# Gate and value projections as seven block products in one pass over 576-token batches, in a fused attention and feed-forward kernel

## The chip, the cores and the metric

The kernel runs on one core of a Trainium2 chip. A core has TensorE (PE; PEld are its weight loads), VectorE (DVE), ScalarE (ACT), GpSimd (POOL) and SyncE (SP), which issues most DMAs. Each engine works through its own queue in order and waits for others by semaphores. The metric is the device time of one execution in microseconds (us), the median of several runs.

## What is computed

Eight batches of eight heads with 576 tokens go through a linear attention. Its output, laid out as 4608 tokens of 512 features, goes through a gated feed-forward block:

```python
def phi(x):
    proj = np.einsum('bhsd,df->bhsf', x, w_phi)
    proj = proj - np.max(np.abs(proj), axis=-1, keepdims=True)
    return np.concatenate([np.exp(proj), np.exp(-proj)], axis=-1)
q_p, k_p = (phi(q), phi(k))
kv = np.einsum('bhsf,bhsd->bhfd', k_p, v)
z = np.sum(k_p, axis=2)
num = np.einsum('bhsf,bhfd->bhsd', q_p, kv)
den = np.einsum('bhsf,bhf->bhs', q_p, z)[..., None] + 1e-06
attn = num / den
...
rms = np.sqrt(np.mean(x * x, axis=-1, keepdims=True) + 1e-06)
xn = x / rms * rms_g
g = xn @ w_gate
silu = g * (1.0 / (1.0 + np.exp(-g)))
val = xn @ w_val
return (silu * val @ w_out).astype(np.float32)
```

`w_gate` and `w_val` are 512 x 1536, `w_out` is 1536 x 512.

## The kernel before

Every operand of the large products is split in two (`_split`): ScalarE casts it to a reduced format ("hi"), and VectorE or GpSimd computes the remainder ("lo"). A product then takes three matmuls in place of one: hi x hi, hi x lo, lo x hi. The weights come in as 64-bit floats and are decoded (`_decode`) by ScalarE, VectorE and GpSimd to 32-bit ones, which go to DRAM (`wgs`, `wvs`, `wos`).

There are three stages, one after the other, with DRAM buffers between them.

1. **Attention** (`front`, `mid`, `back`, `last`), 32 pairs of heads as a software pipeline. It writes its output, transposed, to `xs`. In its gaps lies **fill** (`fill`, called from the loop over the pairs by `landed` and `load_x`): for blocks of T = 384 tokens that are ready, the first three of the twelve 128-wide slices of gate and value are computed from the unnormalised x, with weights `wf1`, and stored in `gvs`. Ten of the twelve blocks are filled there, two (`tail`) in the next stage. One unit of fill is twelve matmuls of 384 columns, a copy by ScalarE and a store.
2. **Gate/value**, the loop over `bk` (12 blocks of 384 tokens) and `j` (nine remaining slices). `gv(bk, j)` computes gate and value of a slice by twelve matmuls each (four parts of the 512 features, three matmuls per part), into banks `fp` and `gp`. `hidden` applies Silu on ScalarE, the product on VectorE, and stores to `hs`. `gv_raw` loads one of the three filled slices back from `gvs`, scales it by the norm `ri` and stores it the same way. `prep` makes the norm of the next block: squares on ScalarE and sums on GpSimd in turn, two matmuls with ones for the sum over partitions, root on ScalarE, reciprocal on VectorE, scaling by g and ri on VectorE, and the split into one of three buffers `xo`. It is called four or two units into a block for the block after. The weights of slice j+1 are loaded and split during the first block (`load_gv`, DMAs issued on ScalarE); the decoding of `w_out` runs in later blocks.
3. **Output** (from `hload`): 18 groups of 256 tokens. The product with `w_out` is done as 2 x 2 blocks by seven block products instead of eight, a scheme of Strassen and Winograd. `load_o` makes the combined weights (four block differences `wc` on VectorE, then splits `wh`, `wl`), `operands` the combined inputs (a11, a12, s1 to s4, a22), and `omm` issues one product of 18 matmuls of 256 columns. Four of the six weight sets are made in stage 2, two at the start of stage 3.

The order on each engine is set by the framework: it takes the instructions in the order in which the program names them and moves later ones forward where its own timing model says that they would be ready. The helper `late()` holds against that: an instruction issued inside it may not stand ahead of the last earlier instruction on its engine (ScalarE, VectorE, GpSimd).

## Time and profile before

| | us |
|---|---|
| median of 3 runs | 1379.31 (1377.8 to 1383.53) |
| the profiled execution | 1376.67 |
| its span, first to last instruction | 1374.9 |
| first and last gate/value matmul | 567.4, 1087.3 |
| first matmul of the output stage | 1097.3 |

The mean granted TensorE clock is 0.976. Rows of the profile read like this: a group has its line, engine and operation, then output <- inputs by the program's names, partitions x elements, the count, the busy time and the mean of one in ns, and the idle time of the engine ahead of it with what ended it. In the view of one line or tile, the three numbers after the count are the shortest, the median and the longest in ns, followed by the first and the last start in us. A timeline row is start, length, engine, line, operation, with the count of instructions merged into it; the step from one start to the next tells the pace, since matmuls overlap. The chain is the work that ended last, followed back through what released it.

### The profile page before, as it was taken

The numbers are of one execution on the slowest core, as the hardware profiler recorded it, in microseconds if no ns is written. First come the engines' busy times: TensorE is split into PE (matmuls) and PEld (weight loads), VectorE is DVE, ScalarE is ACT, GpSimd is POOL, SyncE is SP. The second block draws the span as 40 slices with busy tenths as digits, with TensorE's granted clock in tenths as the row PEclk, the third lists the DMA queues.
The fourth block names the chain that finished last, engine by engine and source line by source line (L and its number), as shares of the span: only waits on it lengthen the run. The fifth ranks groups of instructions, "written<-read, shape, count | busy, mean of one in ns | idle before, by whom it ended". The sixth has DMA issues, their size and how long they took to land.

```text
span 1374.9 us, 24771 instructions
## 1 busy us (share of the span) xinstructions
PE 1300.6 (95%) x9108; PEld 1284.4 (93%) x9108; DVE 880.2 (64%) x1293; ACT 713.3 (52%) x1490; POOL 605.5 (44%) x580
## 2 busy tenths in 40 slices
PE   7988999999999899889999999999999789999998
...
GB/s 165 123 139 127 153 185 149 163 141 171 151 188 153 149 154 119 157 194 129 144 97 167 140 155 132 127 140 157 147 127 98 162 122 127 135 173 131 151 149 47
DMA packets 198953, 197.18 MB, mean 143 GB/s; under 512 B 69104, under 2 KB 180848, under 8 KB 198832
## 3 DMA queue, kind: packets, MB, share of 16 engines
...
q8 instruction: 72, 1.18, 0.4%
...
## 4 chain that ended last, share of the span: by engine, by line
PE 65%; DMA 14%; DVE 12%; issue 3%; ACT 2%; POOL 2%; SPq 1%; ACTq 0%; DVEq 0%; POOLq 0%
PE fp L575 9%; PE gp L575 9%; PE fp L472 7%; PE gd L742 5%; PE gy L742 5%; PE gz L742 5%; PE acc L352 5%; DMA x<-xs 5%; DMA gvr<-gvs 3%; PE sm L416 3%; PE fp L742 3%; PE fp L416 2%; PE pp L314 2%; PE pp L312 2%; PE pp L313 2%
## 5 line engine op out<-in xcount | busy, mean ns | idle before, releaser
L575 PE MATMUL fp<-xo,wg 128*128 128x384 f32 x1296 | 247.4, 339 | 14.7 <-ACT sl L560 14.5
L381 POOL TENSOR_TENSOR ql<-eq,qh 128x256 fp32r<-128x256 f32 x256 | 218.5, 884 | 83.7 <-issue 48.6
L575 PE MATMUL gp<-xo,wv 128*128 128x384 f32 x1296 | 246.6, 338 | 6.3 <-DVE wv L61 5.2
L575 PEld LDWEIGHTS fp<-xo,wg 128*128 128x128 f32 x1296 | 229.2, 190 | 18.0 <-ACT sl L560 17.9
L575 PEld LDWEIGHTS gp<-xo,wv 128*128 128x128 f32 x1296 | 230.3, 191 | 7.3 <-DVE wv L61 5.6
L316 DVE TENSOR_REDUCE mx<-pp 128x4 f32<-128x512 f32 (+1 forms) x160 | 101.1, 633 | 62.8 <-PE pp L314 61.4
L352 PE MATMUL acc<-vm,ek 128*128 128x65 f32 x1024 | 132.5, 268 | 0.0
L560 ACT ACTIVATE sl<-fp 128x384 f32<-128x384 f32 x108 | 52.6, 487 | 153.1 <-PE fp L575 126.2
L54 POOL TENSOR_TENSOR wa<-raw,wa 128x192 f32<-128x192 f32 (+1 forms) x112 | 65.1, 601 | 150.9 <-DVE wa L52 70.3
L562 DVE TENSOR_TENSOR h<-sl,gp 128x384 f32<-128x384 f32 x108 | 59.1, 549 | 110.6 <-PE gp L575 67.6
L352 PEld LDWEIGHTS acc<-vm,ek 128*128 128x128 f32 x1024 | 129.0, 193 | 0.0
L61 POOL TENSOR_TENSOR xo<-x,xo 128x768 fp32r<-128x768 f32 x24 | 44.6, 1878 | 190.7 <-ACT xo L60 190.7
L377 ACT ACTIVATE qh<-sm 128x512 fp32r<-128x512 f32 (+1 forms) x192 | 96.6, 503 | 0.0
L472 PE MATMUL fp<-xo,fg 128*128 128x384 f32 x432 | 90.8, 346 | 3.2 <-ACT xo L60 3.0
L312 PE MATMUL pp<-wh,th 128*128 128x256 f32 x288 | 89.2, 311 | 3.3 <-DVE yr L319 2.1
L376 ACT ACTIVATE eq<-sm 128x512 f32<-128x512 f32 x128 | 78.1, 610 | 17.3 <-PE sm L365 16.8
L583 DVE TENSOR_TENSOR gvr<-gvr,ri 128x768 f32<-128x768 f32 x36 | 38.0, 1056 | 72.7 <-DMA gvr<-gvs 72.7
L314 PE MATMUL pp<-wh,tl 128*128 128x256 f32 x288 | 84.2, 299 | 0.0
L313 PE MATMUL pp<-wl,th 128*128 128x256 f32 x288 | 82.0, 286 | 0.0
L472 PEld LDWEIGHTS fp<-xo,fg 128*128 128x128 f32 x432 | 75.6, 192 | 4.2 <-ACT xo L60 3.3
L472 PE MATMUL fp<-xo,fv 128*128 128x384 f32 x360 | 77.1, 346 | 0.7 <-ACT nd L418 0.7
L383 POOL TENSOR_TENSOR ql<-eqr,qh 128x256 fp32r<-128x256 f32 x32 | 24.7, 772 | 119.0 <-ACT qh L377 119.0
...
## 6 DMA issues: line engine op xcount, KB each, us to landing
...
```

Of the source, the lines that this page charges most:

```text
L312: nc.tensor.matmul(o, th[:, cs], wh, start=True, stop=False)
L313: nc.tensor.matmul(o, th[:, cs], wl, start=False, stop=False)
L314: nc.tensor.matmul(o, tl[:, cs], wh, start=False, stop=True)
L316: nc.vector.tensor_reduce(mx[:, 0:2 * m], pp[:, 0:2 * m], axis=AX.X, op=ALU.max, apply_absolute_value=True)
L352: nc.tensor.matmul(acc[:, sg, h], e[h][:, sg, j], vm[:, h, j], start=False, stop=(h == 1 and j == T0 - 1))
L376: nc.scalar.activation(ei[:, sg], yi, AF.Exp, scale=1.0 - 2.0 * sg)
L377: nc.scalar.activation(hi[:, sg], yi, AF.Exp, scale=1.0 - 2.0 * sg)
L381: nc.gpsimd.tensor_tensor(lo[:, sg, cs], ei[:, sg, cs], hi[:, sg, cs].bitcast(F32), ALU.subtract)
L416: nc.tensor.matmul(o[:, 0:SH], a[:, h, sg], e[:, sg, h, cs], start=(i == 0), stop=(i == 5))
L472: nc.tensor.matmul(fp, w, xx[x][:, c], start=(i == 0), stop=(i == 3 * NC - 1))
L575: nc.tensor.matmul(gp[:, 0:T], w, e[:, c], start=(i == 0), stop=(i == 3 * NC - 1))
L742: nc.tensor.matmul(place[n], a[:, kp], w[:, o], start=(first and kp == 0 and i == 0), stop=(kp == KP - 1 and i == 2), skip_group_check=True)
```

## The change

Stage 2 is replaced. A block is now a whole batch, T2 = 576 tokens, as two halves of T = 288, and a unit computes gate and value of one slice for all 576 tokens at once. Of the matrix [gate, value] by [first, second half of the features] by [first, second half of the tokens] the same seven block products are formed as in stage 3: seven products of six matmuls with 288 columns in place of four times twelve for the same area. The combined weights of all nine slices are made once, in the first batch (`combos`), and stay on chip in fixed places (`home`), 18 tiles of 7 x 256 columns. Partial sums gather in a bank `x` by accumulation, with ScalarE taking snapshots between products (`snap`), and banks `y` and `z` are added on VectorE (`plus`). The last two products of a unit (3 and 4) are issued among the first ones of the next unit.

The combined inputs of the next batch are made around the border of two batches into single buffers, each as soon as the last product that reads the old one is past. The norm of the next batch (`norm`) is issued in `late()` after unit 7 of nine; its sums are on VectorE now, and squares, their sum and `ri` have one buffer each. Fill works on blocks of 288: 14 in the attention stage, two in the first batch; its splits are inside `late()`, and two blocks can be loaded ahead. The raw slices come back in pieces of 288 tokens, six a batch, with one buffer. The decoding of `w_out` is done as twelve pieces of 512 columns in batches 1 to 6, each right behind its load. The weight sets of stage 3 take the places of used gate/value weights in the last batch, whose slices go in the order `LAST`. In stage 3 the remainder of s2 moves from GpSimd to VectorE, the other four are halved, and s2 and s4 are formed in place.

```diff
-    T = 384
+    T = 288
+    T2 = 2 * T
     NB = N // T
     KP = NJ // 2
     DH = DM // 2
-    CH = 256
...
+    SLOT = [128, 7, DH]
+    rga = ctx.enter_context(tc.tile_pool(name="rga", bufs=1, side="right"))
+    slot = lambda n, i, pool: pool.tile(SLOT, F32R, name=f"w{'hl'[i]}{n}")
+    flat = lambda t, n: t.rearrange("p a b -> p (a b)")[:, 0:n]
+    wf1 = [[flat(slot(7 + wi, i, rga), NC * J1 * 128).rearrange("p (c j) -> p c j", c=NC) for i in range(2)] for wi in range(2)]
...
+    def norm(x, bank):
+        ss = xm.tile([128, T2], F32, name="ss")
+        for c in range(NC):
+            sq = ss if c == 0 else xm.tile([128, T2], F32, name="sq")
             nc.scalar.activation(sq, x[:, c], AF.Square)
+            if c:
+                nc.vector.tensor_tensor(ss, ss, sq, ALU.add)
+        ri = xm.tile([128, T2], F32, name="ri")
+        for b in range(2):
+            bs = slice(b * T, (b + 1) * T)
+            s2 = xm.tile([128, 2, T], F32R, name="sq")
+            _split(nc, s2[:, 0], s2[:, 1], ss[:, bs])
+            sp = bank()[:, 0:T]
+            nc.tensor.matmul(sp, ones, s2[:, 0], start=True, stop=False)
+            nc.tensor.matmul(sp, ones, s2[:, 1], start=False, stop=True)
+            nc.scalar.activation(ri[:, bs], sp, AF.Sqrt, scale=1.0 / DM, bias=eps)
+            nc.vector.reciprocal(ri[:, bs], ri[:, bs])
         for c in range(NC):
             nc.vector.scalar_tensor_tensor(x[:, c], x[:, c], g[:, c:c + 1], ri, ALU.mult, ALU.mult)
+        return ri
...
-            else:
-                units.extend(fill(bk, *halves(x)))
+            xo = px.tile([128, 2, NC, T], F32R, name="xo")
+            with late():
+                units.extend(fill(bk, *halves(x, xo[:, 0], xo[:, 1])))
...
         if i == PR - 6:
-            fills.insert(0, None)
+            xn = fetch(0)
+        if i == PR - 3:
+            with late():
+                ri = norm(xn, lambda: ps_f.tile([128, T], F32, name="fp"))
...
+    def combos(n, w, t):
+        sub = lambda o, a, b: nc.vector.tensor_tensor(t[:, o], a, b, ALU.subtract)
+        sub(0, w[:, 3], w[:, W11])
+        sub(2, w[:, W22], w[:, 3])
+        sub(1, w[:, W22], t[:, 0])
+        sub(3, w[:, W21], t[:, 1])
+        wh, wl = home(n, 0), home(n, 1)
+        _split(nc, wh[:, 0:3], wl[:, 0:3], w[:, 0:3])
+        _split(nc, wh[:, 3:7], wl[:, 3:7], t)
+        return wh, wl
+    def stage_gv(j):
+        js = slice((J1 + j) * 128, (J1 + j + 1) * 128)
+        w, t = (stg.tile([128, 4, DH], F32, name="wc") for _ in range(2))
+        for src, os in ((wgs, (W11, W21)), (wvs, (3, W22))):
+            v = src[:, js].rearrange("(k c p) j -> k p c j", k=2, p=128)
+            for k, o in enumerate(os):
+                nc.scalar.dma_start(out=w[:, o].rearrange("p (c j) -> p c j", c=2), in_=v[k])
+        return w, t
+    def decode_o(job):
+        src, n, keep = job
+        raw, tmp = (stg.tile([128, 4, DH], F32, name="wc").rearrange("p a b -> p (a b)") for _ in range(2))
+        if src.dtype == F32:
+            nc.sync.dma_start(out=raw[:, 0:n], in_=src)
+            keep(raw[:, 0:n])
+            return
+        nc.sync.dma_start(out=raw.bitcast(I32), in_=src.bitcast(I32))
+        with late():
+            keep(_decode(nc, None, raw.bitcast(I32).rearrange("p (n t) -> p n t", t=2), n, tmp))
...
+    def operands(a11, a12, a21, a22, tile_of, tmp):
+        ops, t = {}, {}
+        def split(name, x, lo):
+            h, l = tile_of(name)
+            nc.scalar.copy(h, x)
+            m = x.shape[1] // 2
+            for c in (slice(0, m), slice(m, 2 * m)) if lo is nc.gpsimd else (slice(0, 2 * m),):
+                lo.tensor_tensor(l[:, c], x[:, c], h[:, c].bitcast(F32), ALU.subtract)
+            ops[name] = h, l
+        def sums():
+            t["s3"] = tmp()
+            nc.vector.tensor_tensor(t["s3"], a11, a21, ALU.subtract)
+            nc.vector.tensor_tensor(a21, a21, a22, ALU.add)
+            nc.vector.tensor_tensor(a11, a21, a11, ALU.subtract)
+        def second():
+            split("s2", a11, nc.vector)
+            nc.vector.tensor_tensor(a12, a12, a11, ALU.subtract)
+        return ops, [lambda: split("a11", a11, nc.vector),
+                     lambda: (split("a12", a12, nc.vector), sums()), second,
+                     lambda: split("s3", t["s3"], nc.gpsimd), lambda: split("s1", a21, nc.gpsimd),
+                     lambda: split("s4", a12, nc.gpsimd), lambda: split("a22", a22, nc.gpsimd)]
+    def product(n, ops, w, out, start):
+        (xh, xl), o = ops[OPS[n][0]], OPS[n][1]
+        i = 0
+        for c in range(2):
+            for a, e in ((w[0], xh), (w[0], xl), (w[1], xh)):
+                nc.tensor.matmul(out, a[:, o, c * 128:(c + 1) * 128], e[:, c], start=(start and i == 0), stop=(i == 5),
+                                 skip_group_check=True)
+                i += 1
+    class Unit:
+        def __init__(self, p, j, ops, w):
+            self.p, self.j, self.ops, self.w = p, j, ops, w
+        def mm(self, n):
+            out, start = {1: ("x", True), 2: ("z", True), 6: ("x", False), 7: ("y", True), 5: ("x", False),
+                          3: ("x", False), 4: ("y", False)}[n]
+            if start:
+                t = ps_f.tile([128, T], F32, name="fp") if out == "x" else ps_g.tile([128, 512], F32, name="g" + out)
+                setattr(self, out, t[:, 0:T])
+            product(n, self.ops, self.w, getattr(self, out), start)
+            getattr(self, f"done{n}", lambda: None)()
+        def snap(self, name, bufs=1):
+            t = gw.tile([128, T], F32, name=name, bufs=bufs)
+            nc.scalar.copy(t, self.x)
+            return t
+        def plus(self, ps, s, name, bufs=1):
+            t = gw.tile([128, T], F32, name=name, bufs=bufs)
+            nc.vector.tensor_tensor(t, ps, s, ALU.add)
+            return t
+        def store(self, b, x, y, eng):
+            h = gw.tile([128, T], F32, name="h", bufs=3)
+            eng.tensor_tensor(h, x, y, ALU.mult)
+            n0 = self.p * T2 + b * T
+            nc.sync.dma_start(out=hsv[:, J1 + self.j, n0:n0 + T], in_=h)
+        def done1(self):
+            self.s1 = self.snap("s1")
+        def done2(self):
+            self.g1 = self.plus(self.z, self.s1, "g1", 2)
+            nc.scalar.activation(self.g1, self.g1, AF.Silu)
+        def done6(self):
+            self.s2 = self.snap("s2", 2)
+        def done5(self):
+            self.v2 = self.plus(self.y, self.snap("s4"), "v2")
+        def done3(self):
+            self.store(0, self.x, self.g1, nc.vector)
+        def done4(self):
+            g2 = self.plus(self.y, self.s2, "g2")
+            nc.scalar.activation(g2, g2, AF.Silu)
+            self.store(1, g2, self.v2, nc.gpsimd)
+    def raw_fetch(p, j, b):
+        n0 = p * T2 + b * T
+        r = gw.tile([128, 2, T], F32, name="gvr")
+        nc.sync.dma_start(out=r, in_=gvv[j][:, :, n0:n0 + T])
+        return r, b, j, n0
+    def raw_chunk(r, b, j, n0):
+        with late():
+            nc.vector.tensor_tensor(r, r, ri[:, b * T:(b + 1) * T].unsqueeze(1).broadcast_to([128, 2, T]), ALU.mult)
+            nc.scalar.activation(r[:, 0], r[:, 0], AF.Silu)
+            h = gw.tile([128, T], F32, name="h", bufs=3)
+            nc.gpsimd.tensor_tensor(h, r[:, 0], r[:, 1], ALU.mult)
+            nc.sync.dma_start(out=hsv[:, j, n0:n0 + T], in_=h)
+    JN = NJ - J1
+    TAIL = 5
+    LAST = [0, 1, 2, 3, 6, 4, 5, 7, 8]
+    bank = lambda wi: ps_g.tile([128, 512], F32, name="gyz"[0] + "yz"[wi])
+    nbank = lambda: ps_g.tile([128, 512], F32, name="gd", bufs=1)
+    ws, wos_ops, staged = {}, [], {0: stage_gv(0), 1: stage_gv(1)}
+    ops, todo = splits(xn)
+    for piece in todo:
+        piece()
+    todo = []
+    def take(j):
+        with late():
+            ws[j] = combos(j, *staged.pop(j))
+        if j + 2 < JN:
+            staged[j + 2] = stage_gv(j + 2)
+    take(0)
+    prev, raws, ostage = None, None, []
+    for p in range(B):
+        js = LAST if p == B - 1 else range(JN)
+        nops = None
+        for n, j in enumerate(js):
+            if p == 0 and n == TAIL - 1:
+                xt = fetch(B - 1)
+            if p == 0 and n == TAIL:
+                for b, bk in enumerate(tail):
+                    hl = [flat(home(TAIL + b, i), NC * T).rearrange("p (c t) -> p c t", c=NC) for i in range(2)]
+                    with late():
+                        halves(xt[:, :, b * T:(b + 1) * T], *hl)
+                    _merge([fill(bk, *hl, lambda: gw.tile([128, T], F32, name="h", bufs=3))])
+                    if b == 0:
+                        take(TAIL)
+            u = Unit(p, j, ops, ws[j])
+            u.mm(1)
+            if n == JN - 1 and p + 1 < B:
+                nops, todo = splits(xn)
+            do = lambda: todo and todo.pop(0)()
+            if n == JN - 1:
+                do()
+            u.mm(2)
+            if n == JN - 1:
+                do()
+            if p == 0 and n + 1 < JN and n + 1 != TAIL:
+                take(n + 1)
+            if prev:
+                prev.mm(3)
+            if n == 0:
+                do()
+            u.mm(6)
+            if n == JN - 1:
+                do()
+            if prev:
+                prev.mm(4)
+            if n == 0:
+                do()
+            u.mm(7)
+            if n == JN - 1:
+                do()
+            u.mm(5)
+            if n == JN - 1:
+                do()
+            if raws:
+                raw_chunk(*raws)
+            raws = raw_fetch(p, n // 2, n % 2) if n < 2 * J1 else None
+            if p + 1 < B:
+                if n == (TAIL if p == 0 else 1):
+                    xn = fetch(p + 1)
+            if p + 1 < B and n == JN - 2:
+                with late():
+                    nri = norm(xn, nbank)
+            if p and n in (3, 5) and decs_late:
+                decode_o(decs_late.pop(0))
+            if p == B - 1:
+                while len(ostage) < 2 and len(wos_ops) + len(ostage) < KP and n >= 1:
+                    ostage.append(stage_o(len(wos_ops) + len(ostage)))
+                if ostage and len(wos_ops) < KP and len(wos_ops) in js[:n]:
+                    with late():
+                        wos_ops.append(combos(len(wos_ops), *ostage.pop(0)))
+            prev = u
+        if p + 1 < B:
+            ops, ri = nops, nri
+    prev.mm(3)
+    prev.mm(4)
+    assert not decs_late
+    while len(wos_ops) < KP:
+        if not ostage:
+            ostage.append(stage_o(len(wos_ops)))
+        wos_ops.append(combos(len(wos_ops), *ostage.pop(0)))
...
+    OPLACE = dict(s2=(6, 0), s3=(6, 1), s1=(7, 0), s4=(7, 1), a22=(8, 0))
+    def o_tile(name):
+        n = KP * 128
+        if name in OPLACE:
+            t = flat(home(*OPLACE[name]), 2 * n)
+        else:
+            t = xof.tile([128, 2 * n], F32R, name=name)
+        return [t[:, i * n:(i + 1) * n].rearrange("p (k t) -> p k t", k=KP) for i in range(2)]
+    o_tmp = lambda: ost.tile([128, KP, 128], F32, name="st")
```

195 lines of the change are left out of this document (44 added, 151 removed).

## The prediction

> **What bounds the kernel now.** I read the page's busy shares and the shares of the chain first, then a table of stages, and then single stretches of the timeline.
>
> ```profile
> PE 1300.6 (95%) x9108; PEld 1284.4 (93%) x9108; DVE 880.2 (64%) x1293; ACT 713.3 (52%) x1490; POOL 605.5 (44%) x580
> ...
> PE 65%; DMA 14%; DVE 12%; issue 3%; ACT 2%; POOL 2%; SPq 1%; ACTq 0%; DVEq 0%; POOLq 0%
> ```
>
> TensorE is the bound: 95% busy, 65% of the chain. But a busy matmul row is not a matmul at its pace, so I count matmuls by stage.
>
> ```profile
> 150.00:450.00 300.00, 293.86 (x2239) 290.73 (x2239) 213.00 (x358) 216.36 (x519) 148.71 (x182) 0.99 0.57 161
> ...
> 567.00:610.00 43.00, 34.12 (x172) 33.47 (x171) 23.69 (x34) 18.83 (x31) 1.20 (x1) 0.88 0.70 209
> ...
> 1088.00:1111.00 23.00, 8.84 (x49) 7.86 (x50) 18.51 (x19) 8.26 (x10) 8.97 (x4) 0.71 0.56 180
> 1111.00:1370.00 259.00, 258.34 (x2221) 258.13 (x2219) 190.75 (x175) 104.10 (x138) 190.48 (x86) 0.99 0.43 133
> ```
>
> The columns are span, PE, PEld, DVE, ACT and POOL busy (instructions), clock, DMA share, GB/s. The attention stage (to 567) and the output stage (from 1111) have TensorE full. The start of gate/value (567 to 610) and the passage to the output stage (1088 to 1111) have not, and their clock is lower. Next, the pace of a matmul at three widths, each as the step between starts:
>
> ```profile
> 904.55 2.24 PE L575 MATMUL fp<-xo,wg 128*128 128x384 f32 x12
> 906.63 2.24 PE L575 MATMUL gp<-xo,wv 128*128 128x384 f32 x12
> ...
> 1138.46 4.16 PE gy L742 x36
> 1142.63 4.16 PE gz L742 x36
> ...
> 315.00 0.29 PE L416 MATMUL sm<-qh,kv1h 128*128 128x288 f32 x1
> ...
> 315.66 0.30 PE L416 MATMUL sm<-qh,kv1l 128*128 128x288 f32 x1
> ```
>
> 384 columns: 2.08 us for 12, 0.173 each. 256: 4.17 for 36, 0.116. 288 (the third pair is the first and last of six): 0.66 over five steps, 0.132. The pace goes by columns even at 256, so weight loads set no floor at 288. The Trainium skill, "TensorE: Matmul & The Clock Gate", section "Back-to-back issue gap", gives N/2.4 + 2.5 ns, so 162 ns at 384 and 122 at 288, from which the new gate/value products would be an estimated 29 us shorter than below. The rows show 173 and 132; they decide.
>
> ```profile
> L575 PE MATMUL gp<-xo,wv x1296: 334/334/686, 567.4 to 1087.3; 128*128 128x384 f32 x186
> ...
> L742 PE MATMUL fp<-wh,a11h x108: 276/277/582, 1097.3 to 1356.3; 128*128 128x256 f32 x108
> ...
> 1365.18 4.17 PE gd L742 x36
> ```
>
> Gate/value lasts from 567.4 to 1087.6, 520.2 us. Its matmuls at pace are 2592 x 0.173 = 449, two tail fills of 72 are 25, the row sums of the norm 4: 478, so **42 us are lost**. Then come 9.7 us of gap, 2268 x 0.116 = 262.6 within 272.0 of output stage (9.5 lost), and 5.5 to the end of the span.
>
> **The change part by part.** *Fill.* 14 blocks of 288 lie in the attention stage, 14 x 72 x 0.132 = 133.1, in place of 10 x 72 x 0.173 = 124.8: +8.3, where TensorE is full. The tail is 2 x 72 x 0.132 = 19.0 in place of 25. Two block buffers, a start right after the first batch and splits that may not be moved forward spare stalls that are part of the 6 us idle in 150 to 450. I take 6 off (bounds 0 and 10). The copies and splits there are as many columns as before, on engines that are 70% busy: nothing, or some 5 us if VectorE ran late. Gate/value then starts at 569.7.
>
> *Products.* 8 batches x 9 units x 42 matmuls = 3024 x 0.132 = 399.2 in place of 449: **50 us saved**, and with the tail 56. One product of six is 0.79 us, a unit of seven 5.54.
>
> *The border of two batches.* Here I see the price. The norm of the next batch is tied behind everything that unit 7 has given ScalarE and VectorE, so it cannot start before the last product of unit 7 is out and its snapshot taken. The next batch cannot start before the norm and its block sums are done. Between the two TensorE has unit 8 and the leftovers of unit 7 and 8: nine products, 7.1 us. Before, the norm lay several units ahead, and finished operands had spare buffers. The lengths:
>
> ```profile
> L155 ACT ACTIVATE sq<-x x36: 506/525/574, 401.0 to 1018.1; 128x384 f32<-128x384 f32 x36
> L60 ACT CAST a11h<-ht x18: 831/834/846, 1096.4 to 1342.3; 128x768 fp32r<-128x768 f32 x18
> L475 ACT COPY fo<-fp x66: 460/482/560, 158.7 to 681.1; 128x384 f32<-128x384 f32 x66
> L164 ACT ACTIVATE ri<-gp,eps x11: 581/582/586, 606.3 to 1033.6; 128x384 f32<-128x384 f32 x11
> L562 DVE TENSOR_TENSOR h<-sl,gp x108: 540/548/558, 591.8 to 1087.7; 128x384 f32<-128x384 f32 x108
> L61 DVE TENSOR_TENSOR a11l<-ht,a11h x18: 943/946/2594, 1097.3 to 1344.9; 128x768 fp32r<-128x768 f32 x18
> L165 DVE RECIPROCAL ri<-ri x12: 2543/2546/2554, 446.8 to 1034.9; 128x384 f32<-128x384 f32 x12
> L167 DVE SCALAR_TENSOR_TENSOR x<-x,g,ri x48: 604/614/1105, 450.7 to 1039.1; 128x384 f32<-128x384 f32 x48
> ...
> 772.46 1.04 POOL L156 TENSOR_TENSOR ss<-ss,sq 128x384 f32<-128x384 f32 x1 [0.64 <-ACT sq L155]
> 773.54 0.53 ACT L155 ACTIVATE sq<-x 128x384 f32<-128x384 f32 x1 [1.16 <-POOL ss L156]
> 774.14 1.01 POOL L156 TENSOR_TENSOR ss<-ss,sq 128x384 f32<-128x384 f32 x1 [0.64 <-ACT sq L155]
> ```
>
> Between the widths shown I go in a straight line. ScalarE (0.525 at 384, 0.834 at 768): 0.45 at 288, 0.68 at 576. VectorE with two inputs (0.548, 0.946): 0.45 and 0.75. Reciprocal at 288: 1.91. Scaling of 576 columns: 0.81. Root and snapshot, by width: 0.47 and 0.4. The last three rows show that square and add take turns, since the square's tile has one buffer; it still has one. From the end of unit 7's last product:
>
> - snapshot with the drain 0.65; four squares and three adds in turn 2 x 0.68 + 0.75 + 2 x (0.68 + 0.75), and 0.5 for six handovers: at 6.1.
> - first half: cast 0.45, remainder 0.45, two matmuls and handovers 0.75, root 0.47, reciprocal 1.91: at 10.1.
> - second half: its short steps beside the first reciprocal or behind it, then 1.91: at 12.0 to 13.5.
> - four scalings 3.2: at 15.2 to 16.7; the cast of a11 lies beside, its remainder (0.75) behind, and the first new product needs it with its second matmul: 16.0 to 17.5.
> - a12's remainder 0.75, three sums 2.25, cast and remainder of s2 1.43, handovers 0.3: product 6 of the new unit at 20.7 to 22.2; this and products 7 and 5 end at 23 to 24.5.
>
> To that point TensorE has 14 products, 11.1 us. The loss is 12 to 13.4 us, and units 7 and 8 still put six VectorE steps of 0.45 in between. I take **13 us a border, 91 for seven**. The bounds: 7 (only the wait for the first product, 16 less 9, were the block sums wholly covered) and 17 (unit steps in between, second half behind). Behind these waits on VectorE stand the product of unit 8's two stores and so their DMAs on SP; nobody else waits for these. GpSimd is out of the norm now.
>
> After such an idle stretch the clock is low:
>
> ```profile
> 1097.26 0.58 PE L742 MATMUL fp<-wh,a11h 128*128 128x256 f32 x1 [9.64 <-ACT a11h L60]
> ...
> 1099.03 0.41 PE L742 MATMUL fp<-wl,a11h 128*128 128x256 f32 x1
> 1099.24 0.41 PE L742 MATMUL fp<-wh,a11l 128*128 128x256 f32 x1
> ```
>
> After 9.64 us of idling the step is 0.21 in place of 0.116. At a border the first products wait for VectorE anyway, so I charge nothing more than lies within the 13. The Trainium skill, "TensorE: Matmul & The Clock Gate", section "What's actually happening", says that one idle window of about 3.4 us halves the clock until a busy window has passed. By that rule every border would add up to half a window, an estimate of 12 us in all; the row agrees with the halving.
>
> *First batch.* Every unit now needs its weights combined:
>
> ```profile
> L602 DVE TENSOR_TENSOR wc<-wc x24: 412/424/2050, 732.9 to 1109.1; 128x256 f32<-128x256 f32 x24
> L61 DVE TENSOR_TENSOR wl<-wc,wh x12: 946/1082/2040, 750.0 to 1111.2; 128x768 fp32r<-128x768 f32 x6, 128x1024 fp32r<-128x1024 f32 x6
> ...
> L555 ACTq DMA_DIRECT2D wc<-wgs x9: 366/367/680, 547.1 to 597.0; - x9
> ```
>
> 4 x 0.42 + 2 x 1.08 = 3.9 on VectorE, with the unit's own four steps of 0.45 and a raw block of 0.75 6.4, some 7.3 when GpSimd runs beside (the maxima of the rows): 1.8 over a unit, 14 for eight, less 4 that the tail fill covers. The loads, now four a unit, are issued on ScalarE, 4 x 0.37 = 1.5, beside casts of 1.9 and five unit steps of 0.4 to 0.45: 5.5 of 7.3, hidden behind VectorE. With 7 to get going I take 17 (8 to 30). Before, 172 matmuls or 30 us of work lay in the 43 us from 567 to 610, so 13 were lost there too.
>
> *Waits for DMAs.*
>
> ```profile
> DVE gvr L583 <- DMA gvr<-gvs: 72.7, 31, 5.8
> ...
> ACT ss L152 <- DMA x<-xs: 50.5, 10, 6.2
> ...
> 736.46 3.15 DMA gvr<-gvs
> ```
>
> The wait of the norm for x goes: the fetch is now six units ahead (in SP's queue at unit 1, where its buffer has just come free, so no store stands long behind it). The raw blocks are 48 in place of 36, still with one buffer, and their loop is 0.75 VectorE, 0.45 ScalarE, some 0.8 GpSimd, 0.4 issue, 3.15 DMA and handovers: 5.8, just over a unit. VectorE waits in order for it, the unit's own sums behind it, and TensorE for those. The 12 decodings wait on ScalarE for a load issued just before, the snapshots behind it, which TensorE needs 1.6 us later. I take 20 for both; bounds 0 and 60 (72.7 over 31 is 2.3 a wait, half of it through to TensorE for 48).
>
> *Output stage.* All weights are ready, so their part of the 9.5 lost goes; the gap stays, since the load of h is still issued behind the last store:
>
> ```profile
> 1089.68 1.27 SPq L713 DMA_DIRECT2D ht<-hs  x2
> ...
> 1096.38 0.96 DVE L677 TENSOR_TENSOR st<-ht 128x768 f32<-128x768 f32 x1 [1.18 <-DMA ht<-hs]
> ```
>
> The last store comes later by a sum, a Silu and a GpSimd product. I take 11 and 5 in place of 9.7 and 9.5. A remainder goes from GpSimd to VectorE: 18 x 0.95 on 191 busy of 259, hidden behind full TensorE; without that cover it would be 17 us.
>
> **The sum.** 569.7 + 399.2 + 19.0 + 17 + 91 + 20 = 1115.9 for the end of gate/value; + 11 + 262.6 + 5 + 5.5 = 1400. That is 25 above the span of 1374.9, so 1376.67 + 25 = 1402; the median shown, 1379.31, is 3 higher than the profiled execution, and I stay at 1402.
>
> **The rivals.** *The border is covered* (faster). If the second reciprocal's half and the block sums slip between the first ones, the border costs 7, the sum falls by 42 to 1360, and to 1345 if the raw loop keeps up as well. It decides below 9.5 a border (25 / 7 less than 13). For it: the norm before was spread among other work at no cost to TensorE. Against: single buffers, and two reciprocals that nothing shortens. 0.27.
> *Even*: borders of 9 to 10: 1379. 0.13.
> *The raw loop paces the units* (slower still): 60 in place of 20, 1442. For it the 72.7 us row; against it that TensorE waited little then. 0.12.
> *The products do not do what they say*, weight loads as a floor: excluded by 0.116 at 256.
> The forecast, borders of 11 to 15: 0.48.
>
> **How the numbers follow.** Faster 0.27, within 0.5% (about what a measurement of this kernel can tell) 0.13, slower 0.60. The forecast alone spans 1386 to 1420; with the rivals the range is 1345 to 1440.
>
> **What would show it.** Right: in the changed profile seven idle stretches of TensorE, each some 7 us and a few more behind it, one per batch, ended by the cast or remainder of a11 and s2, with the clock row low there, and matmuls of 288 at 0.132. Wrong: TensorE without gaps between batches, or gaps that end on gvr. If the step at 288 is not 0.132, the 50 us saved are wrong.

## The result and the profile after

The changed kernel is **slower**: 1434.58 us median of four runs (1432.18 to 1440.22) against 1378.55 (1376.94 to 1383.53) for the kernel before on the same chip, ratio 1.0406 with a 95% interval of 1.0365 to 1.0447. That is 56 us; the forecast had 23. The profiled execution took 1435.34 us, its span is 1433.5. The page of the changed kernel, busy times and chain:

```profile
PE 1293.3 (90%) x9836; PEld 1255.8 (88%) x9836; DVE 981.1 (68%) x1547; ACT 835.5 (58%) x1792; POOL 665.6 (46%) x722
...
PE 27%; issue 6%; DVE 6%; POOL 5%; DMA 4%; ACT 3%; SPq 1%; POOLq 0%; ACTq 0%; DVEq 0%
```

TensorE is busy 7 us less than before, in a span 59 us longer. The shares of the chain add up to 52%: it is followed back only to 707 us, so its 27% can't be set against the 65% before. In the part of gate/value that it covers, 707 to 1156, TensorE holds 110 of 449 us; before, it held 276 of 515 (575 to 1090). The rest now passes through all engines in turn. I set the stages apart by the timeline: a batch begins with the first matmul on its new a11. The table of windows (columns as in the prediction) shows batches 0, 1, 4 and 7 and the output stage:

```profile
574.16:667.93 93.77, 77.22 (x527) 72.17 (x527) 62.16 (x107) 48.40 (x95) 14.84 (x15) 0.95 0.49 142
667.93:738.53 70.60, 57.40 (x383) 54.10 (x383) 40.37 (x69) 35.67 (x74) 24.73 (x27) 0.91 0.38 115
878.04:947.66 69.62, 56.91 (x383) 53.31 (x383) 40.41 (x69) 35.70 (x74) 24.80 (x27) 0.92 0.38 117
1087.30:1156.02 68.72, 57.04 (x379) 53.21 (x380) 50.97 (x87) 38.45 (x74) 28.94 (x26) 0.95 0.40 125
1156.02:1433.50 277.48, 272.54 (x2268) 272.34 (x2267) 196.15 (x197) 106.62 (x141) 175.25 (x142) 0.99 0.41 132
```

A batch has 9 x 42 matmuls, 378 x 0.132 = 49.9 us of products, and takes 70: batches 1 to 6 lose 20 us each. Batch 7, which has no next batch to prepare, loses 18.8; batch 0 holds the tail fill (19.0) as well and loses 25. Now one border, on TensorE:

```profile
878.04 0.85 PE L651 MATMUL fp<-a11h,wh 128*128 128x288 f32 x2 [5.46 <-ACT a11h L618]
879.50 0.85 PE L651 MATMUL gz<-a12h,wh 128*128 128x288 f32 x2 [0.61 <-ACT a12h L618]
...
881.50 0.44 PE L651 MATMUL fp<-a11l,wh 128*128 128x288 f32 x1
881.74 0.44 PE L651 MATMUL fp<-a11h,wl 128*128 128x288 f32 x1
...
883.90 0.30 PE L651 MATMUL gz<-a12l,wh 128*128 128x288 f32 x1
884.03 0.29 PE L651 MATMUL gz<-a12h,wl 128*128 128x288 f32 x1
...
885.34 0.40 PE L651 MATMUL gy<-s3l,wh 128*128 128x288 f32 x1 [0.35 <-POOL s3l L621]
```

An idle stretch of 5.46 us ends on the cast of a11, and behind it the step between starts is 0.24 us, half the clock; from 883.90 on it is 0.13. The other side of the same border, VectorE and then ScalarE:

```profile
862.74 0.46 DVE L677 TENSOR_TENSOR v<-gy,s 128x288 f32<-128x288 f32 x1 [1.91 <-POOL h L682]
863.12 0.75 DVE L156 TENSOR_TENSOR ss<-ss,sq 128x576 f32<-128x576 f32 x1
...
866.12 0.76 DVE L156 TENSOR_TENSOR ss<-ss,sq 128x576 f32<-128x576 f32 x1 [0.38 <-ACT sq L154]
...
869.86 1.95 DVE L166 RECIPROCAL ri<-ri 128x288 f32<-128x288 f32 x1 [0.20 <-ACT ri L165]
871.73 0.39 DVE L64 TENSOR_TENSOR sq<-ss,sq 128x288 fp32r<-128x288 f32 x1
873.75 1.95 DVE L166 RECIPROCAL ri<-ri 128x288 f32<-128x288 f32 x1 [1.62 <-ACT ri L165]
875.74 3.00 DVE L168 SCALAR_TENSOR_TENSOR xn<-xn,g,ri 128x576 f32<-128x576 f32 x4
...
883.28 1.35 DVE L621 TENSOR_TENSOR s2l<-xn,s2h 128x576 fp32r<-128x576 f32 x1
```

```profile
859.20 0.38 ACT L672 COPY s<-fp 128x288 f32<-128x288 f32 x1
859.48 0.69 ACT L154 ACTIVATE ss<-xn 128x576 f32<-128x576 f32 x1
...
870.16 1.28 ACT L704 ACT_TABLE_LOAD   x1
871.46 0.44 ACT L704 ACTIVATE g<-g 128x288 f32<-128x288 f32 x1
871.92 1.28 ACT L165 ACT_TABLE_LOAD   x1
873.21 0.50 ACT L165 ACTIVATE ri<-gd,eps 128x288 f32<-128x288 f32 x1
```

The last snapshot of unit 7 (859.20) marks the end of its last product, from which the prediction counted. From there the sums of squares end at 7.7 us (forecast 6.1), the first reciprocal at 12.6 (10.1), the second at 16.5 (12.0 to 13.5), the scalings at 19.5 (15.2 to 16.7); the first new product begins at 18.8 (16.0 to 17.5) and s2 is ready at 25.4 (20.7 to 22.2). The first of the three adds begins at 863.12, although its square was ready at 860.74: a sum of a unit stood ahead of it on VectorE and waited 1.91 us for a product on GpSimd. Between the two reciprocals lie 1.9 us in which VectorE does the second half's remainder, which stood behind the first reciprocal, and then waits for a root that stands behind a Silu with a table load on either side.

The middle of a batch, in the chain of waits:

```profile
835.62 3.34 DMA gvr<-gvs
...
838.98 0.77 DVE gvr L715
...
839.84 0.46 ACT gvr L716
...
840.36 1.10 POOL h L718
...
847.78 3.81 DMA gvr<-gvs
```

One raw block goes round through DMA, VectorE, ScalarE and GpSimd before the next reload may begin, since all share one buffer. In this batch the scalings of raw blocks start 6.0 to 8.1 us apart, where TensorE's work for a unit is 5.54.

So there are two suspects, the **border** and the **raw loop**, and the first experiments leave out one, the other and both.

### The profile page after: what moved, and what is told of

Read it like the earlier page. It is cut to its first block, busy times and chain, and to the rows that moved or that the text cites. A ratio compares the mean times of both kernels' runs of the same rounds, so it can differ in the third digit from the quotient of the medians.

```text
span 1433.5 us, 27130 instructions
## 1 busy us (share of the span) xinstructions
PE 1293.3 (90%) x9836; PEld 1255.8 (88%) x9836; DVE 981.1 (68%) x1547; ACT 835.5 (58%) x1792; POOL 665.6 (46%) x722
## 3 DMA queue, kind: packets, MB, share of 16 engines
q8 instruction: 78, 1.28, 0.4%
## 4 chain that ended last, share of the span: by engine, by line
PE 27%; issue 6%; DVE 6%; POOL 5%; DMA 4%; ACT 3%; SPq 1%; POOLq 0%; ACTq 0%; DVEq 0%
PE gz L885 6%; PE gd L885 5%; PE gy L885 5%; PE fp L651 4%; PE gy L651 3%; PE fp L885 3%; DMA gvr<-gvs 2%; POOL h L682 1%; POOL a22l L621 1%; DVE xn L168 1%; DMA hs<-h 1%; PE gz L651 1%; POOL h L718 1%; DVE ri L166 1%; DVE g L677 1%
## 5 line engine op out<-in xcount | busy, mean ns | idle before, releaser
L484 PE MATMUL fp<-xo,wh 128*128 128x288 f32 x672 | 147.3, 306 | 5.3 <-DVE xo L64 3.4
L672 ACT COPY s<-fp 128x288 f32<-128x288 f32 x216 | 85.2, 395 | 114.5 <-PE fp L651 109.7
L682 POOL TENSOR_TENSOR h<-g,v 128x288 f32<-128x288 f32 x72 | 64.1, 890 | 147.0 <-ACT g L704 121.4
L718 POOL TENSOR_TENSOR h<-gvr 128x288 f32<-128x288 f32 x48 | 45.7, 951 | 156.5 <-ACT gvr L716 141.4
L484 PEld LDWEIGHTS fp<-xo,wh 128*128 128x128 f32 x672 | 111.0, 193 | 6.4 <-DVE xo L64 3.7
L484 PE MATMUL fp<-xo,wl 128*128 128x288 f32 x336 | 100.7, 300 | 0.0
L677 DVE TENSOR_TENSOR v<-gy,s 128x288 f32<-128x288 f32 x72 | 32.8, 456 | 87.8 <-POOL h L682 49.7
L621 POOL TENSOR_TENSOR wh<-ht,wh 128x384 fp32r<-128x384 f32 x72 | 89.9, 1269 | 3.1 <-ACT wh L618 0.9
L651 PE MATMUL fp<-a11h,wh 128*128 128x288 f32 x144 | 48.1, 344 | 47.1 <-ACT a11h L618 37.3
L618 ACT CAST wh<-ht 128x768 fp32r<-128x768 f32 x54 | 45.0, 835 | 71.4 <-PE gz L885 20.7
L340 ACT ACTIVATE ek<-yk 128x512 f32<-128x512 f32 x128 | 74.7, 645 | 2.5 <-PE acc L353 1.3
```

The costliest lines, as they stand in the source:

```text
L484: nc.tensor.matmul(fp, w, xx[x][:, c], start=(i == 0), stop=(i == 3 * NC - 1))
L621: lo.tensor_tensor(l[:, c], x[:, c], h[:, c].bitcast(F32), ALU.subtract)
L651: nc.tensor.matmul(out, a[:, o, c * 128:(c + 1) * 128], e[:, c], start=(start and i == 0), stop=(i == 5), skip_group_check=True)
L672: nc.scalar.copy(t, self.x)
```

## The experiments

All edits are to the changed kernel. The kernel before took 1374.62 to 1379.53 us beside these runs, on different chips, and the runs without an interval are single executions, so a difference to the changed kernel's 1434.58 that is under some 5 us is not resolved. Part of that spread is the start of gate/value, which lies between 570.2 and 576.6 us in runs that share the attention stage. Batches are measured as above; the changed kernel has 93.8 us in batch 0, 69.9 on average in 1 to 6, 68.7 in 7.

**Without the norm, without the raw work, without both.**

```diff
-                with late():
-                    nri = norm(xn, nbank)
+                nri = ri
```

> Leaves out the RMS norm of batches 1 to 7 (squares, row sums, roots, the scaling of x; batch 0's factors are used again), so seven of the eight batch borders keep the operand splits and lose the chain before them. Changed kernel: batches 1 to 6 take 69.9 us each against 49.9 for their products alone, batch 7 68.5. Theory 'border': nearly all that the steady batches lose is lost at the border to the norm chain, 14 to 16 us of 20, so the batches fall to 54 to 56 us and the run by 7 x 14 = 98 us, to about 1335. Theory 'raw loop': the one-buffer reload of raw gate/value blocks sets the pace inside the batch and the border only collects its delay, so at most 5 to 8 us a batch go, 35 to 55 us in all, to about 1390. Both: batch 7, which has no norm of its own, stays at 68 us.

Measured 1321.41 us, **113 less**. Batches: 77.7, 54.9, 64.3. Batch 7 fell by 4.4 although the norm issued in it is none: the last border's late operands reach into it. Its first 60 matmuls take 7.8 us here and 11.8 in the changed kernel. Of the 113 us, 2 are an earlier start, which the edit doesn't explain.

```diff
-            nc.sync.dma_start(out=gvv[j][:, wi, bk * T:(bk + 1) * T], in_=o)
+            dst = gvv[j][:, wi] if wi else hsv[:, j]
+            nc.sync.dma_start(out=dst[:, bk * T:(bk + 1) * T], in_=o)
...
-            raws = raw_fetch(p, n // 2, n % 2) if n < 2 * J1 else None
+            raws = None
```

> Leaves out the finishing of the raw gate/value columns inside the batches (48 reloads, scalings by the norm, Silus, products and stores); the fill writes its gate output to the hidden rows instead. Theory 'raw loop': the six reloads of a batch, 6.0 to 8.1 us apart against 5.54 us of TensorE work in a unit, cost 5 to 9 us a batch in batches 1 to 6 and nearly all of batch 7's 18.6 us, which has no border: batch 7 falls from 68.5 to about 53 us, the run by 50 to 75 us, to about 1365. Theory 'border': batches 1 to 6 lose 2 us each at most, batch 7 stays above 64 us (its other work, the combined output weights, sets it), the run falls by 10 to 20 us, to about 1420.

Measured 1398.53, **36 less**; batches 86.2, 66.0, 65.4. Neither theory's numbers hold: batches 1 to 6 gain 4 each, more than "border" allowed and less than "raw loop" did, and batch 7 stays at 65, as "border" had it.

> Leaves out both the norm of batches 1 to 7 and the finishing of the raw columns. If the two costs are separate, the gains of the two runs before add (about 98 + 50 = 150 us, to 1285, batches 1 to 6 at 50 to 51 us). If each hides behind the other, the gain here is larger than their sum; if they are one and the same delay, it is no more than the larger of the two. What is left above 49.9 us a batch belongs to neither.

Measured 1289.92, 145 less; batches 73.9, 51.2, 57.7. The windows of batches 4 and 7 in this run:

```profile
798.77:849.02 50.25, 50.25 (x380) 50.05 (x379) 25.62 (x52) 23.66 (x56) 18.09 (x21) 1.00 0.33 109
953.82:1011.48 57.66, 52.00 (x382) 51.07 (x380) 41.52 (x81) 33.29 (x67) 17.29 (x20) 0.96 0.38 123
```

Batch 4 runs at the pace of its products, at full clock, TensorE busy throughout: splits and block sums cost nothing when norm and raw work are gone. The two costs add (113 + 36 = 149 for 145). Batch 7 keeps 7.8 us, for which VectorE's 41.5 us busy (25.6 in batch 4) is the hint.

**The same work in another place.** The norm of batches 1 to 6 behind unit 4, with a second tile for its factors:

```diff
-            if p + 1 < B and n == JN - 2:
+            if p + 1 < B and n == (JN - 2 if p == 0 else 4):
                 with late():
-                    nri = norm(xn, nbank)
+                    nri = norm(xn, nbank, lambda dt: gw.tile([128, 2, T], dt, name="st"), ("sq", "ri")[p % 2])
```

> Computes everything: in batches 1 to 6 the norm of the next batch is issued behind unit 4 instead of behind unit 7, with a second tile for its factors and squares in a tile that is free there; batch 0 keeps the old place. Theory 'border' (the chain stands on the path only because it begins behind unit 7): six of seven borders lose 12 to 14 us, the run falls by 60 to 85 us, to about 1360, below the kernel before. Theory 'raw loop' (VectorE and ScalarE are paced, so the chain's work costs the same wherever it stands): the run falls by 25 us at most, to 1410 or more, and the gaps between reloads grow from 6 to 8 us to 9 or more behind unit 4.

Measured 1386.48, 48 less, between the two; batches 94.7, 62.1, 66.9. The idle stretches at the six borders are gone, but only half of the gain came: batches 1 to 6 gain 7.8 us each, where leaving the norm out gave 15.0. My next theory was that the chain still stood as one block in the queues, so it was cut into steps:

```diff
+        return ri, {3: [lambda: square(0), lambda: square(1)], 4: [lambda: square(2), lambda: square(3), lambda: cut(0)],
+                    5: [lambda: root(0), lambda: cut(1)], 6: [lambda: root(1)], 7: [scale]}
...
+                for step in steps.get(n, ()) if n > 2 else ():
+                    with late():
+                        step()
```

> Computes everything: the norm of the next batch is cut into five steps of at most some 4 us, put behind units 3 to 7 of batches 1 to 6 (squares behind 3 and 4, the two row sums with their roots behind 5 and 6, one unit after the splits that feed them, the scalings behind 7), with a second tile for the factors. Moving the whole norm behind unit 4 gave 48 us of the 113 us that leaving it out gave. Theory 'place of the chain': what that run still lost (batches of 61.5 us against 54 without the norm) is the chain of 18 us standing as one block in the queues of VectorE and ScalarE; in steps the batches fall to 54 to 56 us, the run to 1335 to 1350. Theory 'work': the norm's 10 us of VectorE and 4 us of ScalarE do not fit beside a unit, wherever they stand: the batches stay at 60 us or more, the run at 1375 to 1390.

Measured 1392.34 (1388.52 to 1394.03), ratio 1.0095 (1.0061 to 1.0128) to before; batches 92.9, 62.7, 68.1. The theory fell: no gain over the single block, and batches above 60, as the rival "work" had it. What TensorE waits for between 740 and 1040 in this run (in total, times, longest):

```profile
PE fp L682 <- ACT s L703: 19.1, 33, 1.2
PE gy L682 <- DVE g L708: 7.7, 7, 1.6
```

Small waits for snapshots and for the sums that free a bank have taken the place of one long one: ScalarE and VectorE come to them late, because the norm's pieces stand ahead. In the run without the norm, TensorE's list of waits from 720 to 975 has none for a snapshot.

**What in the border is long.** Three edits of the norm as it stands behind unit 7: an identity in place of the square root; no reciprocals; a second tile for the second half's cast and remainder.

```diff
-            nc.scalar.activation(ri[:, bs], sp, AF.Sqrt, scale=1.0 / DM, bias=eps)
+            nc.scalar.activation(ri[:, bs], sp, AF.Identity if nbk[0] else AF.Sqrt, scale=1.0 / DM, bias=eps)
```

> Leaves out the square roots of the norms of batches 1 to 7 (an identity with the same operands stands there), and with them ScalarE's table loads at the borders, three of 1.28 us between the two halves and one behind. If the table loads that my forecast had no term for are what made the border 15.5 us rather than 13, the run falls by 7 x 2.5 to 3.8 = 18 to 27 us, to about 1412. If they lie beside the reciprocals, it falls by less than 7 us.

```diff
-            nc.vector.reciprocal(ri[:, bs], ri[:, bs])
+            if not nbk[0]:
+                nc.vector.reciprocal(ri[:, bs], ri[:, bs])
```

> Leaves out the reciprocals of the norms of batches 1 to 7 (14 x 1.95 us on VectorE). If both stand on the chain, as the forecast had them, the run falls by 7 x 3.9 = 27 us, to about 1407; if the roots' table loads of the second half only take their place, by 7 x 2 = 14 us, to about 1421.

```diff
-            s2 = xm.tile([128, 2, T], F32R, name="sq")
+            s2 = second() if second and b else xm.tile([128, 2, T], F32R, name="sq")
```

> Computes everything: the changed kernel with a second tile for the cast and remainder of the norm's second half, so that they need not wait for the row-sum matmuls of the first half. In the changed kernel the second reciprocal ends 17.0 us after unit 7's last product, forecast were 12.0 to 13.5. Theory 'one tile': the second half's cast and remainder then stand ahead of the first reciprocal, the second root follows the first, and a border loses 2 to 3.5 us: minus 14 to 24, about 1415. Theory 'VectorE's queue': unit 8's sums and products and the table loads keep the halves apart all the same: minus 5 us or less.

Measured 1430.87 (minus 4), 1421.88 (minus 13) and 1426.94 (minus 8): each less than the border's rows suggested, the first hardly resolved. The rows say more than the times. At the border into batch 4, counted from the snapshot as above, the second reciprocal ends at 16.1 without the table loads and at 16.2 with the second tile, for 16.5. Without the table loads the first one still ends at 12.8, for 12.6 in the changed kernel, so the load ahead of the first root costs nothing. Without the reciprocals the scalings end 2.0 sooner, the length of one reciprocal: the second root comes when it came before. In the run with the second tile, ScalarE at a border:

```profile
864.04 0.50 ACT L165 ACTIVATE ri<-gd,eps 128x288 f32<-128x288 f32 x1 [0.34 <-PE gd L164]
864.56 1.28 ACT L704 ACT_TABLE_LOAD   x1
865.85 0.44 ACT L704 ACTIVATE g<-g 128x288 f32<-128x288 f32 x1
866.31 1.28 ACT L165 ACT_TABLE_LOAD   x1
867.61 0.50 ACT L165 ACTIVATE ri<-gd,eps 128x288 f32<-128x288 f32 x1
```

The tile is no longer the reason, and the second root still comes 3.6 us after the first: now it is the Silu with its two tables. Each had covered the other. The last run takes both away, with a tile and a bank for each half:

```diff
+            sums.append((bs, sp))
...
+        for bs, sp in sums:
+            nc.scalar.activation(ri[:, bs], sp, AF.Sqrt, scale=1.0 / DM, bias=eps)
+        for bs, sp in sums:
+            nc.vector.reciprocal(ri[:, bs], ri[:, bs])
```

> Computes everything: the changed kernel with the norm behind unit 7 as it is, but a tile and a bank for each half, so that both casts and remainders come first, then both roots side by side, then both reciprocals. In the run with the second tile alone a Silu with two table loads still stood between the two roots, and 1.6 us passed between the reciprocals. Theory 'two covers': the tile and the table loads each hid behind the other, and with both gone the second reciprocal follows the first at once: 2 us a border there and the wait for the first root's table once more, minus 14 to 24 us against the changed kernel, about 1415. Rival: the two alone gave 8 and 4 us and together give their sum, 12 us or less: 1423 or more.

Measured 1417.52 (1417.28 to 1418.11), **17 less**, 2.4 a border; batches 90.5, 67.5, 68.8. VectorE at a border of this run:

```profile
862.26 3.76 DVE L170 RECIPROCAL ri<-ri 128x288 f32<-128x288 f32 x2 [0.20 <-ACT ri L168]
866.06 3.01 DVE L172 SCALAR_TENSOR_TENSOR xn<-xn,g,ri 128x576 f32<-128x576 f32 x4
```

The reciprocals follow each other without a gap: 3.8 us from the start of the first to the end of the second, 5.8 in the changed kernel. That saves 2 us a border, which is nearly all that the run shows. The second reciprocal ends at 14.4 from the snapshot, 2.1 sooner, where the two edits alone had moved it by 0.4 and 0.3.

**The clock behind the border.** 82 matmuls without use in each norm keep TensorE busy there:

```diff
+            spin(to, 14 * b)
             nc.tensor.matmul(sp, ones, s2[:, 1], start=False, stop=True)
+            spin(to, (8, 60)[b])
```

> Computes everything, and in each of the seven norms TensorE also runs 82 matmuls of 128 columns without use, between and behind the row sums, which fill the idle stretch of the border. Theory 'clock': the halved clock of the first 5 to 6 us of a batch costs some 2.5 us a border, and this wins minus 12 to 19 us, about 1418. Theory 'covered' (the forecast charged nothing): the first products wait for the splits of s3, s2 and a22 whatever the clock, and the change is within 5 us of nothing; if the empty matmuls delay the second row sum or the first product, it is up to 10 us slower.

Measured 1438.55, 4 more. The first products behind the border into batch 4:

```profile
877.62 6.81 PE L154 MATMUL gs<-ones 128*128 128x128 f32 x60
884.26 0.48 PE L659 MATMUL fp<-a11h,wh 128*128 128x288 f32 x2
...
885.57 0.29 PE L659 MATMUL fp<-a11h,wl 128*128 128x288 f32 x1
885.70 0.29 PE L659 MATMUL fp<-a11h,wh 128*128 128x288 f32 x1
...
890.54 0.40 PE L659 MATMUL gy<-s3l,wh 128*128 128x288 f32 x1 [2.03 <-POOL s3l L629]
```

The step is 0.13 from the start now, and TensorE waits 2.03 us for the remainder of s3, where it waited 0.35 at the half clock: what the clock gave, the wait took. At each of the six borders into batches 2 to 7 the empty matmuls held up the first product by 1.0 us, and batches 2 to 6 take 69.8 us, as in the changed kernel. So the full clock gave back that 1.0 us a border and no more, an estimate of 7 for seven. The border into batch 1 came out differently:

```profile
661.87 12.89 PE L154 MATMUL gs<-ones 128*128 128x128 f32 x60
674.56 0.79 PE L659 MATMUL fp<-a11h,wh 128*128 128x288 f32 x2
```

There the clock had halved ahead of the last 60 empty matmuls and stayed at 0.50 through all of them, although TensorE had no idle time. They took 12.89 us in place of 6.81, held the first product 7.7 us behind the cast of a11, and made batch 0 8.0 us longer (101.8), more than the 4 us by which the run is longer. Why the clock didn't come back there stays open.

**The raw loop's buffer.** Every second block goes to the tile of the norm's sums, free until unit 7:

```diff
-        r = gw.tile([128, 2, T], F32, name="gvr")
+        r = gw.tile([128, 2, T], F32, name="gvr") if b == 0 else xm.tile([128, 2, T], F32, name="ss")
```

> Computes everything: every second raw block is reloaded into the tile that holds the norm's sums (free until unit 7), so that the reload no longer waits for the block before. Leaving the whole raw work out gave 36 us. Theory 'one buffer': the loop DMA, VectorE, ScalarE, GpSimd of 6.0 to 8.1 us is what costs, and nearly all of it goes: the run falls by 25 to 35 us, to about 1403. Theory 'work': the 0.75 us of VectorE, 0.43 of ScalarE and 0.8 of GpSimd in six of nine units cost what they take, loop or not: it falls by less than 10 us.

Measured 1400.48 (1397.09 to 1405.31), **34 less**, ratio 1.0169 (1.0128 to 1.0211) to before; batches 89.7, 64.8, 69.4. In total nearly all that leaving the raw work out gave: the cost was the one buffer, not the work. By batches the two runs differ: the second buffer gives 5.1 us in each of batches 1 to 6, leaving the work out 3.9, and in batch 7 the buffer gives nothing, where leaving the work out gave 3. Leaving it out had also changed TensorE's order: 59 matmuls in place of 46 stand between the snapshot and the first new product. The border into batch 4, ScalarE and then VectorE:

```profile
837.48 0.38 ACT L672 COPY s<-fp 128x288 f32<-128x288 f32 x1
...
849.91 1.95 DVE L166 RECIPROCAL ri<-ri 128x288 f32<-128x288 f32 x1 [1.62 <-ACT ri L165]
```

From the snapshot the sums of squares now end at 6.1 us (7.7 before), the first reciprocal at 10.5 (12.6), the second at 14.4 (16.5), and s2 is ready at 23.3 (25.4). So 2.1 of the 5.1 us are won at the border: the raw loop had reached into it. VectorE's waits for reloads in the changed kernel between 575 and 1156 were

```profile
DVE gvr L715 <- DMA gvr<-gvs: 34.5, 31, 2.0
```

and in this run no such wait is among the nine largest.

**TensorE's order, and batch 7.** The order in which TensorE gets the products isn't the written one; the planner re-sorts them. This run ties it to the written order:

```diff
+            if last_mm:
+                es.enter_context(tc.issue_after(last_mm.pop()))
+            product_(*a)
```

> Computes everything: only the order of the products on TensorE is tied to the written one (1, 2, 3 of the unit before, 6, 4 of the unit before, 7, 5). In the changed kernel only one product, 0.79 us, stands between two sums of a unit that share a bank with a snapshot of 0.4 us between them; written are two. Theory 'snapshots': what the middle of a batch loses is TensorE waiting for snapshots; with 1.6 us between them these waits go, but the border has 7 products to fill it instead of 9: minus 8 x 3 plus 7 x 1.6, so 10 to 15 us faster than the changed kernel, about 1422. Theory 'border and raw loop alone': nothing to gain inside, and the border is longer by 1.6 us: 1440 to 1450.

Measured 1424.39, 10 less; batches 92.4, 68.1, 68.9. That is the number of the snapshots theory, but not its way: in gate/value TensorE still waits 17.8 us for snapshots, against 18.9 in the changed kernel. What did change is ScalarE's work at the border: no Silu stands between the two roots, the run has 20 table loads in place of 32, and the second reciprocal follows the first by 3.5 us in place of 3.9. How much of the 10 us that makes isn't shown.

```diff
-                        wos_ops.append(combos(len(wos_ops), *ostage.pop(0)))
+                        ostage.pop(0)
+                        wos_ops.append(ws[len(wos_ops)])
```

> Leaves out the combining and splitting of the output weights in batch 7 (the gate/value combinations stand in for them; their loads stay). With norm and raw work left out batch 7 took 57.7 us against 50 in the others. If the combinations are what is left, batch 7 falls from 68.7 to about 61 us and the run by 7 to 8 us, to about 1427; if they lie beside the raw loop, by 2 us or less.

Measured 1425.17, 9 less. Batch 7 gave 4.6 of it (64.1), where 7 to 8 were expected, the output stage 2.9 (277.5 to 274.6); the rest is a start 2.3 us earlier, which the edit doesn't explain.

**Together.** Norm in steps and second raw buffer; and the same with the written order:

> Computes everything: the norm in five steps and a second buffer for the raw blocks (in batches 1 to 6 one of the weight staging tiles, in 0 and 7 the tile of the norm's sums). Alone they gave 42 and 34 us. If they are separate costs, the run falls by 76 us, to about 1358, and batches 1 to 6 take 57 to 58 us, batch 7 some 63. If the steps lie in the same queues as the raw blocks and it is VectorE's and ScalarE's work beside each unit that holds TensorE, the second buffer gives less than 15 us more and the run stays above 1375.

Measured 1367.25 (1364.70 to 1369.61), ratio 0.9918 (0.9901 to 0.9935): **below the kernel before**. Batches 89.6, 58.8, 69.5; 67 of the 76 us came, so the costs are separate but for 9.

> Computes everything: norm in steps, second raw buffer, and the products of TensorE in the written order. Theory 'snapshots': without a wait at the border the written order only helps, and batches 1 to 6 come to 52 to 54 us: 1320 to 1340. If the shortage is VectorE's and ScalarE's work, not the order, it is within 10 us of the run with the steps and the second buffer alone.

Measured 1407.87 (1406.15 to 1408.67), 41 *more* than without the written order, outside both theories; batches 92.3, 64.6, 72.5. TensorE behind a border of this run:

```profile
801.45 0.40 PE L692 MATMUL fp<-s2h,wh 128*128 128x288 f32 x1 [0.94 <-ACT s2h L649]
804.79 0.61 PE L692 MATMUL fp<-s2l,wh 128*128 128x288 f32 x1 [2.94 <-DVE s2l L652]
```

In the written order product 6, on s2, stands fourth in the new batch, and the remainder of s2 is ready only 8.0 us behind the first product. The planner's order had put products 2 and 7 in front. The waits for snapshots inside the batch didn't go either. In one batch of this run (861.5 to 926.3) they are

```profile
PE fp L692 <- ACT s L713: 3.9, 3, 1.9
```

and 0.7 us in a batch of the run without the written order.

Two more versions carry the steps on. In one, batch 0 gets them too, and GpSimd forms the differences of the output weights:

```diff
-    TAIL = 5
+    TAIL = 2
...
-                        wos_ops.append(combos(len(wos_ops), *ostage.pop(0)))
+                        wos_ops.append(combos(len(wos_ops), *ostage.pop(0), nc.gpsimd))
```

> Computes everything: the norm in steps and the second raw buffer as before, and now in batch 0 as well (its tail fill behind unit 2 rather than unit 5, so that x of batch 1 comes in time), and in batch 7 GpSimd forms the four differences of the output weights instead of VectorE. Batch 0 loses 20.7 us above its products and tail, of which leaving norm and raw work out gave back all but 5; batch 7 lost 8 to 9 us to the combinations. Theory: batch 0 falls by 8 to 12 us, batch 7 by 3 to 5: about 1353. Rival: the tail fill behind unit 2 waits for x of the last batch and GpSimd's differences are slower beside VectorE's work: within 5 us of 1367.

Measured 1358.72 (1358.23 to 1362.78), ratio 0.9884 (0.9855 to 0.9912), against 0.9918 before this step (the two intervals overlap); batches 87.5, 58.9, 68.4. Batch 0 gave 2 us and batch 7 gave 1, far less than expected, and GpSimd's differences spare hardly anything; more than those 3 us can't be traced in the profiles. In the other, the roots are put together and the steps begin a unit earlier:

```diff
+                    4: [lambda: total(0), lambda: cut(1)], 5: [lambda: total(1), roots, lambda: recip(0)],
+                    6: [lambda: recip(1), lambda: scale((0, 1))], 7: [lambda: scale((2, 3))]}
```

> Computes everything: as the run before, with the norm's steps one unit earlier (behind units 2 to 7), the two roots side by side (two banks for the row sums, so two table loads a norm fewer), the two reciprocals in different units and the scalings in two parts. Theory 'blocks': of the 8 us a batch that the steps still lose, most lies behind units 6 to 8, where roots, reciprocal and scalings stand ahead of the sums that free the banks; in smaller pieces 3 to 5 us a batch go, about 1330. Rival 'work': what ScalarE and VectorE have to do for the norm delays snapshots wherever it stands: within 7 us of the run before.

Measured **1345.97** (1344.92 to 1346.98), ratio 0.9792 (0.9767 to 0.9816) to the kernel before, the fastest here: 2.1% below it, 89 us below the changed kernel. Batches 86.5, 57.0, 68.0; a window of a steady batch:

```profile
774.25:829.68 55.43, 52.59 (x385) 50.91 (x383) 40.41 (x69) 32.78 (x72) 24.08 (x27) 1.00 0.48 151
```

That is 13 us less than the run before, between the two theories: more than "work" allows, but 1.9 a batch where "blocks" had 3 to 5. VectorE is as busy as in the changed kernel's batch 4 (40.4), ScalarE 3 us less (32.8 for 35.7), in a batch that is 14 us shorter.

## Why the prediction came out as it did

The direction and the place were right, the size was not: 1402 forecast, 1434.58 measured, inside the range. The step that failed is **the border**, 91 us in the sum and 113 by the run without the norm. Two things in it were wrong: the way to the first reciprocal, which the raw loop held up, and the norm's two halves, which I let run side by side and which ran one behind the other. Beside it the raw loop was under-sized, and 16 us that batches lose elsewhere had no term. By terms, span against span (1400 forecast, 1433.5 measured):

| term | forecast | measured | how |
|---|---|---|---|
| start of gate/value | 569.7 | 574.2 | timeline |
| products, tail | 399.2 + 19.0 | the same | step 0.132 |
| borders | 91 | 113 | norm left out |
| DMA waits (raw loop) | 20 | 31 to 36 | raw work left out, with and without the norm |
| first batch | 17 | 5 | both left out: 73.9 less 49.9 and 19.0 |
| batch 7 above its products | none | 8 | both left out: 57.7 less 49.9; output weights alone 4.6 |
| six other batches | none | 8 | both left out: 6 x (51.2 less 49.9) |
| output stage with gap and end | 284 | 277.5 | window |

With 31 to 36 in the fourth row the differences add up to 35 to 40 us, for 33.5; some of the costs overlap, the raw loop's part in the border among them.

- *Products at 0.132, a start at half clock, seven idle stretches of 4.9 to 5.5 us ended by the cast of a11*: right; the rows show them.
- *Four squares and three adds at 6.1, the first reciprocal at 10.1.* Late by 2.5: steps of units 7 and 8, and the waits of these steps, got in between the squares and adds (1.6) and ahead of the root (0.9). I had them only in the upper bound, 17. With the second raw buffer the two points lie at 6.1 and 10.5, so most of this was the raw loop, which I had taken as a cost apart from the border. A table load stands ahead of the root, for which my sum had no term, but it cost nothing there.
- *The second half's short steps lie beside the first reciprocal or behind it, its own ends at 12.0 to 13.5.* This failed: 16.5, and 3.9 us behind the first where I had 1.9 to 3.4. One tile for both halves put the second remainder behind the first reciprocal, and a Silu brought two more table loads between the roots, for which the sum had no term. With the halves together the second is 1.8 behind the first, 2.1 us a border sooner, which is most of the 17 us of that run; the single edits each left the other cover in place. The rest of the sum held: scalings 3.0 for 3.2, from there to s2 5.9 for 5.5. By 113 / 7 the border is 16.1, as s2, 3.2 us later than the latest I had, says too.
- *At a border the half clock costs nothing more than lies within the 13*: near enough. At the borders with a full clock, in the run with the empty matmuls, the gain was some 1.0 us each, an estimate of 7 for all seven. The Trainium skill, "TensorE: Matmul & The Clock Gate", section "What's actually happening", agrees with the rows on the halving. The 12 us estimated from it were not to be had, because the remainders of s3 and s2 came no sooner. That a busy window ends the halving doesn't hold at the border into batch 1 of that run: 12.7 us of matmuls without idle time left the granted clock at 0.50.
- *DMA waits 20*: under-sized, and one of its two parts was not there: waits of the decoding for its load don't show among the large waits. All of it is the raw loop. I set its round at 5.8 us, just over a unit; it is 6.0 to 8.1 in the batch shown. The rival "the raw loop paces the units" had 60, and was half right.
- *First batch 17*: over-sized. Four combinations beside each unit hid but for 5 us.
- *Batch 7*: not in the sum. I moved the output weights to "all weights are ready" in the output stage (a gain that came, 6.5 us below forecast there) and charged nothing for combining them where they went.
- *Start 569.7*: 574.2, but the runs that share this attention stage start between 570.2 and 576.6, so this term is hardly resolved. A wait of 3.4 us stands at the end of the fill; it doesn't explain the 4.5, since in the run that starts at 570.2 it is 4.8.
- *The border is covered* (the faster rival) decided below 9.5 a border; measured is 16. (Its lower sum was 5 off: 1360 less the raw loop's 20 is 1340, not 1345.) Against it spoke what I named, single buffers and the reciprocals. But moving the norm gave back only half of what it cost: 7.8 and 7.2 us in each of batches 1 to 6, of 15.0. The other half is the norm's work on VectorE and ScalarE beside the units, in both places tried, shown as small waits for snapshots. How it divides between the two engines stays open; with the roots together, the steps earlier and the raw blocks in two buffers, a batch still lies 6 us above the one without norm and raw work (57.0 against 51.2).
